# Chunk 4 of two head pairs scored in one visit on four array tiles, chunks 2 and 3 in one visit, masks ahead of the scores, one transposition for chunks 0 and 1, new ranks

## Chip, core and metric

The kernel runs on one core of a Trainium2 chip. The metric is the time of one execution on the device in microseconds (us), lower is better; it is the median of several runs. A measurement of this kernel tells a difference of about 1% from none.

## What is computed

Attention with a compressive memory, gated, and behind it a feed-forward layer with softplus, all in float32 at the interface:

```python
scores = scale * q @ k.T                       # B,H,S,D = 4,8,576,64; causal
a = exp(scores - rowmax); a /= a.sum(-1) + 1e-9
local = a @ v
mem_out = (phi(q) @ M_prev) / (phi(q) @ z_prev + 1e-6)   # phi = elu + 1
x = g * mem_out + (1 - g) * local              # g = sigmoid(beta), per head
out = softplus(x @ w_in) @ w_out               # 2304 tokens, 512 -> 2048 -> 512
```

## The kernel before

**Units, windows, chunks.** Two heads form a unit, each on 64 partitions; there are 4 batches of 4 units. A unit's 576 queries fall into window A (chunks 0 and 1, 128 queries each) and window B (chunks 2 and 3 of 128 queries, chunk 4 of 64). A batch is worked as four windows A, then four windows B; together 32 windows, numbered by `win.no`. The list `halves` has them in this order.

**One window.** `memory` (L771) computes phi(q) on ScalarE and GpSimd (L780 to L792), multiplies it with M and z on TensorE (L800) and divides on VectorE (L807 to L813). `chunks` (L503) computes the scores: for chunks 0 to 3 four float32 matmuls each, 64 rows by 64 columns of the array (L529: two heads by two halves of the queries), and behind them one bf16 matmul for each head that adds the causal mask (L540 for chunks 0 and 1 together, L544 for chunk 2 or 3). Chunk 4 holds 64 queries only: GpSimd first lays both heads' queries into a 128x128 tile `qz` with zeros elsewhere (L571), and two float32 matmuls of the full array over the 576 keys (L533) and one mask matmul (L535) follow. Then the row maximum on VectorE (L549, L552), the exponential with its row sum on ScalarE (L560, L564), the reciprocal (L595, L597), the split of the probabilities into two float16 halves on GpSimd and VectorE (L617 to L656, tile `PHL`), and a transposition of `PHL` by DMA on SyncE's queue into `PTA` or `PTB` (L630: one for each of chunks 0 to 3; L664: two for chunk 4). In windows 0 to 6 (`PEH`) the transposition is done by TensorE instead (`turned`, L715) and copied out (L724). `values` (L820) multiplies the transposed probabilities with v (L838, or L853 in windows 0 to 6), adds the memory part, and stores the window's part of x as `xhl`.

**Feed-forward layer.** A block is one batch's windows A (256 tokens) or B (320 tokens), eight blocks in all. `fill` (L898) takes a finished block through the first 7 of 16 slices of the weights (L384, `h<-xhl,w` and `h<-g,w`) while attention goes on with later windows, and stores the part sum. `rest` (L921) does the last block whole and then what is left of the others, when attention is done (L384 and L951). The weights come as 64-bit words and are decoded (`decode`, L466) by VectorE, GpSimd and ScalarE; slices 0 to 6 during the first batch, slices 7 to 15 when the tiles of attention are free. The decoding ends with L317 on GpSimd.

**What sets the order.** The functions only register operations (`op`) with an engine, a planned duration, a rank and the tiles that they read and write. `Plan.run` (L148) then goes through them as a list scheduler and writes the order of each engine, which is fixed from then on. Ranks come from the slot of a window's chunk and the tables `SLOT`, `RK`, `DEC`; `OPT` chooses the engine of some operations and the lead of the loads (`pf`). Where the plan sees a gap on TensorE in the early part, it puts matmuls on `ident` whose result is not used (L1034, "fillers" below). Scores and the transpositions on TensorE share a ring `s` of two tiles.

Of the kernel before, what the change touches and what calls it, by code (L numbers as in the profile page):

```python
# [10 lines left out]
F32 = mybir.dt.float32  # L11
# [21 lines left out]
DEC = {(0, 0): -99.18, (1, 0): -54.775, (2, 0): -197.277, (3, 0): 33.228, (4, 0): 45.246, (5, 0): 305.867, (6, 0): 52.475, (0, 1): -63.029, (1, 1): -24.184, (2, 1): -157.376, (3, 1): -80.924, (4, 1): -116.755, (5, 1): 28.921, (6, 1): -155.375}  # L33
PELO = {(0, 1), (4, 0), (2, 1), (1, 1), (2, 0), (5, 1), (3, 0), (1, 0), (4, 1)}
PHS = 10
RK = {'qz': -30.021, 'v': 36.457, 'mem': 2.9, 'prod': 16.414, 'norm': 34.649, 'r': -35.845, 'hi': -54.718, 'lo': -42.164, 'vhi': -2.071, 'vlo': -26.791, 'val': -9.765}
SLOT = {0: -12.775, 3: -66.133, 20: -22.329, 2: -24.201, 24: -137.226, 8: -16.423, 17: -94.807, 13: 41.989, 12: -82.022, 5: -57.35, 27: -24.194, 9: -20.573, 6: 30.327, 23: -262.096, 26: 144.982, 29: 129.289, 22: -36.136, 16: -1.399, 10: 75.094, 21: -4.617, 14: -88.782, 4: -45.41, 15: -80.316, 28: -160.775, 7: -8.892, 19: 14.465, 25: 7.92, 1: -139.922, 11: 30.92, 18: 74.083, 30: -27.465, 31: 120.802}
PARTS = {'A': [[0, 1]], 'B': [[2], [3], [4]]}
ORDER = [0, 1, 2, 3, 4, 5, 6]
PEH = {0, 1, 2, 3, 4, 5, 6}  # L40
OPT = {'rp': {0, 2, 3, 6, 7, 8}, 'hp': {8, 11, 12}, 'ev': {0, 6, 7, 13, 17, 19, 20, 23, 26}, 'pf': -20.780194481621944, 'hold': 1.5519182956108535, 'ab': {1, 2, 4, 5, 6, 7, 8, 9, 10, 11, 12, 13, 14, 15}, 'gp': set()}
# [53 lines left out]
class Plan:  # L95
# [5 lines left out]
    TURN = {"m": {"S": 60.0, "v": 160.0, "n": 70.0}, "f": {"v": 85.0}, "n": {"S": 30.0, "v": 80.0},  # L101
            "S": {"S": 85.0, "v": 80.0, "f": 90.0, "m": 90.0, "n": 90.0},
            "v": {"S": 80.0, "f": 90.0, "m": 90.0, "n": 90.0}}
# [44 lines left out]
    def run(self):  # L148
# [34 lines left out]
        def opens(o):  # L183
            t = 0.0
            for h in o.tiles:
                if h.ring is None or h.open:
                    continue
                if h.ring.free:
                    if h.before is not None and not h.before.open:
                        return None  # L190
                    if len(h.ring.opened) >= h.ring.bufs:
                        old = h.ring.opened[-h.ring.bufs]
# [80 lines left out]
def attn_softplus_moe(  # L273
# [25 lines left out]
    own = res.tile([128, 128], F32, name="own")  # L299
# [86 lines left out]
    def consts():  # L386
# [11 lines left out]
        P.memset(own, 0.0)  # L398
        for h in range(2):
            P.memset(own[64 * h:64 * h + 64, 64 * h:64 * h + 64], 1.0)  # L400
# [9 lines left out]
        for r in range(2):  # L410
            V.tensor_copy(cinv4[64 * r:64 * r + 64, :], cv[64 * r:64 * r + 64, :, r])
# [12 lines left out]
    def ring(pool, tag, bufs, shape, dtype=F32):  # L424
# [18 lines left out]
        "PTA": ring(al, "PTA", 2, [128, 8, 256], F16), "PTB": ring(al, "PTB", 2, [128, 18, 320], F16),  # L443
# [16 lines left out]
    QZ = [Handle(None, 0) for _ in range(2)]  # L460
    for i, h in enumerate(QZ):
        h.t = res.tile([128, 128], F32, name=f"qz{i}")
# [40 lines left out]
    def chunks(u, win, b, p, cs, ks):  # L503
# [14 lines left out]
        ss, nms, pts = (tiles(t) for t in ("s", "nm", "P"))  # L518
        l, r = R["l"].new(), R["rr"].new()

        def scores(js):
            for j in js:
                c, n, sv, qv, kv = cs[j], ns[j], ss[j](), q()[:, 130:], kk()
                cq = c * 128 - q0
                if c < 4:
                    for h in range(2):
                        rr = slice(64 * h, 64 * h + 64)
                        for e in range(0, 128, 64):
                            MM(sv[e:e + 64, h, so[j]:so[j] + n], lhsT=qv[rr, cq + e:cq + e + 64], rhs=kv[rr, :n],  # L529
# [562 lines left out]
```

## Time and profile before

| | |
|---|---|
| median of 3 runs | 611.39 us (608.29 to 611.94) |
| the profiled execution | 610.6 us |
| its span, first to last instruction | 608.8 us |
| TensorE busy | 590.4 us |
| VectorE, ScalarE, GpSimd busy | 353.0, 302.4, 173.0 us |
| granted TensorE clock, mean | 1.000 |

The busy time of an engine counts the stretches in which an instruction of it ran. In a timeline, a line merges instructions of one kind in sequence; since matmuls overlap, the cost of one line is read from its start to the start of the next, not from its own duration. A float32 matmul stands there as two instructions. In brackets stands how long the engine was idle before it and what ended that.

### The profile page before, as it was taken

The numbers are of one execution on the slowest core, as the hardware profiler recorded it, in microseconds if no ns is written. First come the engines' busy times: TensorE is split into PE (matmuls) and PEld (weight loads), VectorE is DVE, ScalarE is ACT, GpSimd is POOL, SyncE is SP. The second block draws the span as 40 slices with busy tenths as digits, with TensorE's granted clock in tenths as the row PEclk, the third lists the DMA queues.
The fourth block names the chain that finished last, engine by engine and source line by source line (L and its number), as shares of the span: only waits on it lengthen the run. The fifth ranks groups of instructions, "written<-read, shape, count | busy, mean of one in ns | idle before, by whom it ended". The sixth has DMA issues, their size and how long they took to land.

```text
span 608.8 us, 12824 instructions
## 1 busy us (share of the span) xinstructions
PE 590.4 (97%) x4866; PEld 528.5 (87%) x4866; DVE 353.0 (58%) x805; ACT 302.4 (50%) x854; POOL 173.0 (28%) x262
## 2 busy tenths in 40 slices
PE   6999999999989999989999999999999999999996
PEld 5676768787777787968799999999999999999996
DVE  6688888788877898868882776651212121212121
ACT  5758866666756785668743443432222222222221
POOL 3556533334433435326622343330000000000000
PEclk9999999999999999999999999999999999999999
DMA  8545559868999789967976643342314130522011
GB/s 314 190 125 178 181 157 220 195 195 183 205 180 210 192 187 200 177 164 163 169 123 182 214 137 106 105 145 98 105 36 133 48 132 6 167 71 70 1 44 35
DMA packets 129245, 87.41 MB, mean 144 GB/s; under 512 B 86176, under 2 KB 120992, under 8 KB 129184
## 3 DMA queue, kind: packets, MB, share of 16 engines
q1 hardware_dynamic: 129184, 86.60, 55.3%
q8 instruction: 38, 0.62, 0.4%
q14 instruction: 23, 0.19, 0.1%
HBM read 47.88 MB, written 18.22 MB: 109 GB/s over the span
## 4 chain that ended last, share of the span: by engine, by line
PE 86%; DMA 5%; DVE 4%; ACT 1%; SPq 1%; POOL 1%; issue 1%; DVEq 0%; ACTq 0%; POOLq 0%
PE h L384 43%; PE s L951 21%; PE s L529 6%; PE xp L838 4%; PE sm L800 3%; PE s L533 2%; DMA kA<-in_nat_dram 2%; PE xp L853 2%; PE xp L826 1%; PE s L544 1%; PE h L488 1%; DMA qA<-in_nat_dram 1%; PE s L715 1%; DVE nm L549 1%; DMA PTA<-PHL 1%
## 5 line engine op out<-in xcount | busy, mean ns | idle before, releaser
L384 PE MATMUL h<-xhl,w 128*128 128x256 f32 (+1 forms) x1536 | 228.1, 298 | 1.4 <-ACT pb L914 1.4
L384 PEld LDWEIGHTS h<-xhl,w 128*128 128x128 f32 x1536 | 210.4, 189 | 3.2 <-ACT pb L914 1.6
L317 DVE TENSOR_TENSOR g<-gl,g 128x256 fp32r<-128x256 f32 (+1 forms) x128 | 59.6, 470 | 162.8 <-ACT g L323 162.5
L888 ACT ACTIVATE gl<-h 128x256 f32<-128x256 f32 (+1 forms) x128 | 52.2, 410 | 179.2 <-PE h L384 176.8
L951 PE MATMUL s<-g,w 128*128 128x320 f32 (+1 forms) x948 | 139.3, 297 | 0.0
L951 PEld LDWEIGHTS s<-g,w 128*128 128x128 f32 x948 | 131.1, 188 | 0.0
L384 PE MATMUL h<-g,w 128*128 128x256 f32 (+1 forms) x588 | 87.1, 299 | 0.0
L384 PEld LDWEIGHTS h<-g,w 128*128 128x128 f32 x588 | 78.7, 189 | 0.7
L617 POOL TENSOR_SCALAR PHL<-P,rr 128x384 f16<-128x384 f32 (+3 forms) x100 | 57.4, 589 | 76.9 <-DVE rr L597 23.5
L560 ACT ACTIVATE P<-s,nm 128x256 f32<-128x256 f32 (+3 forms) x128 | 66.4, 526 | 5.2 <-DVE PHL L621 2.6
L549 DVE TENSOR_REDUCE nm<-s 128x2 f32<-128x768 f32 (+2 forms) x64 | 51.4, 818 | 13.9 <-PE s L540 7.3
L323 ACT CAST g<-gl 128x256 fp32r<-128x256 f32 (+1 forms) x128 | 55.1, 433 | 3.9
L621 DVE SCALAR_TENSOR_TENSOR PHL<-P,rr,PHL 128x384 f16<-128x384 f32 (+3 forms) x100 | 56.4, 599 | 0.8 <-POOL PHL L617 0.8
L317 POOL TENSOR_TENSOR w<-wu,w 128x512 fp32r<-128x512 f32 x23 | 30.5, 1329 | 29.2 <-ACT w L323 29.2
L353 POOL TENSOR_SCALAR wu<-wu 128x512 f32<-128x512 f32 x32 | 20.5, 643 | 43.7 <-DVE wu L349 38.3
L529 PE MATMUL s<-kB,qB 64*64 64x384 f32 (+1 forms) x256 | 31.4, 561 | 0.0
L838 PEld LDWEIGHTS <-vb 128*64 128x64 f16 x508 | 24.8, 110 | 7.1 <-issue 2.7
L360 DVE SCALAR_TENSOR_TENSOR wu<-ws,wu 128x512 int32<-128x512 int32 x32 | 26.6, 832 | 0.9
L792 POOL TENSOR_TENSOR ph<-ph,pe 128x320 f32<-128x320 f32 (+1 forms) x22 | 18.4, 838 | 30.8 <-ACT pe L784 18.9
L560 ACT ACTIVATION_READ_ACCUMULATOR P<-s,nm 128x1 f32 x128 | 25.5, 199 | 0.0
L323 ACT CAST w<-wu 128x512 fp32r<-128x512 f32 x29 | 17.9, 618 | 14.4 <-DVE wu L364 14.2
L678 POOL TENSOR_SCALAR P<-P,rr 128x256 f32<-128x256 f32 (+4 forms) x31 | 18.6, 613 | 20.5 <-DVE rr L597 10.7
(123 smaller groups left out, 643.2 us busy)
## 6 DMA issues: line engine op xcount, KB each, us to landing
ws<-in_w_in_dram SPq DMA_DIRECT2D x16, 512.0 KB, 3.6
ws<-in_w_out_dram SPq DMA_DIRECT2D x16, 512.0 KB, 3.5
va<-in_nat_dram SPq DMA_DIRECT2D x16, 320.0 KB, 3.9
xd<-xhl SPq DMA_DIRECT2D x16, 320.0 KB, 3.1
kB<-in_nat_dram SPq DMA_DIRECT2D x16, 288.0 KB, 3.8
xd<-xhl SPq DMA_DIRECT2D x16, 256.0 KB, 3.2
xhl<-xd SPq DMA_DIRECT2D x8, 512.0 KB, 4.6
xhl<-xd SPq DMA_DIRECT2D x6, 640.0 KB, 4.9
```

The source lines that it names most:

```text
L317: eng.tensor_tensor(out=out, in0=in0, in1=in1, op=ALU.subtract)
L323: A.copy(out, in_)
L360: V.scalar_tensor_tensor(out=ti(), in0=si(1), scalar=-0x40000000, in1=ti(), op0=ALU.bitwise_and, op1=ALU.bitwise_or)
L384: MM(out, lhsT=l, rhs=r, start=start and i == 0, stop=stop and i == len(pairs) - 1)
L529: MM(sv[e:e + 64, h, so[j]:so[j] + n], lhsT=qv[rr, cq + e:cq + e + 64], rhs=kv[rr, :n], start=j == js[0], stop=True, skip_group_check=True)
L549: V.tensor_reduce(out=nm()[:, 2 * j * both:2 * j * both + 2], in_=s()[:, :, so[j]:so[j] + n], op=ALU.max, axis=AX.X, negate=True)
L560: A.activation(out=pt()[:, po[j] + h * n:po[j] + h * n + n], in_=s()[:, h, so[j]:so[j] + n], func=AF.Softplus, scale=SCALE, bias=nm()[:, o ...
L617: P.tensor_scalar(out=o[:, :, 0, h, :], in0=src, scalar1=rs, scalar2=0.0, op0=ALU.mult, op1=ALU.add)
L621: V.scalar_tensor_tensor(out=o[:, :, 1, h, :], in0=src, scalar=rs, in1=o[:, :, 0, h, :], op0=ALU.mult, op1=ALU.subtract)
L838: MM(xp()[64 * h:64 * h + 64, lo:n], lhsT=vb()[:, vi, kc, 64 * h:64 * h + 64], rhs=ptw()[:, kc * 4 + t * 2 + h, lo:n], start=False, stop=( ...
L888: op("ACT", 170 + .833 * n, -1, lambda: A.activation(out=gl()[:, :n], in_=hp()[:, :n], func=AF.Softplus, scale=XSC), r=[hp], w=[gl])
L951: MM(bank(dm), lhsT=l, rhs=r, start=f == f0 and q == 0 and (not small or dm % 2 == 0), stop=f == NF - 1 and q == 2, skip_group_check=True)
```

## The change

It does six things. (1) `fours`: chunk 4 of two neighbouring units is scored in one visit of TensorE, eight float32 matmuls of 64x64 with 288 columns, the four tiles of the array taking one head of one unit each; the second unit's heads are swapped (`win.odd`). The tile `qz` and its GpSimd operation go. `values` of the even unit waits for this visit, which is planned with the odd unit's window. (2) `twos`: chunks 2 and 3 in one visit in 14 of the 16 windows B (`OPT['two']`; units 12 and 13 keep two visits); it takes both score tiles. (3) The mask matmuls stand ahead of the scores, in all visits. (4) One DMA transposition for chunks 0 and 1 in place of two, in the 12 windows A that use DMA; `PTA` gets the shape 128x12x128. (5) Windows 10 and 11 add phi's two parts by accumulating matmuls (`PHS` 10 to 12), as windows 0 to 9 do; one block's casts of `g` go from ScalarE to GpSimd (`gp`), two operations of window 30 and 31 from GpSimd to ScalarE. (6) The tables of ranks, the planned durations and the planned costs of switching are new.

```diff
-PHS = 10
+PHS = 12
-PARTS = {'A': [[0, 1]], 'B': [[2], [3], [4]]}
+PARTS = {'A': [[0, 1]], 'B': [[2], [3]]}
...
+    def fours(wins, ks):
+        ss = [R["s"].new() for _ in wins]
...
+        def scores():
+            for s in ss:
+                MM(s()[:, 1, 224:288], lhsT=identb, rhs=mask4, start=True, stop=False, skip_group_check=True)
+            for i in (1, 0):
+                for h in range(2):
+                    rr = slice(64 * h, 64 * h + 64)
+                    for s, w in zip(ss, wins):
+                        o = 64 * (h ^ w.odd)
+                        MM(s()[o:o + 64, i, :288], lhsT=w.q()[rr, 130 + 256:130 + 320],
+                           rhs=w.k()[rr, 288 * i:288 * i + 288], start=i == 0, stop=True, skip_group_check=True)
...
+    def twos(win, ks):
+        ss = [R["s"].new() for _ in range(2)]
...
+        def scores():
+            for c, s in zip((2, 3), ss):
+                for h in range(2):
+                    MM(s()[:, h, c * 128:c * 128 + 128], lhsT=identb, rhs=mask, start=True, stop=False,
+                       skip_group_check=True)
+            for c, s in zip((2, 3), ss):
+                n = c * 128 + 128
+                for h in range(2):
+                    rr = slice(64 * h, 64 * h + 64)
+                    for e in range(0, 128, 64):
+                        MM(s()[e:e + 64, h, :n], lhsT=win.q()[rr, 130 + n + e - 384:130 + n + e - 320],
+                           rhs=win.k()[rr, :n], start=False, stop=True, skip_group_check=True)
...
-                else:
-                    for i in range(2):
-                        MM(sv[:, i, :288], lhsT=win.qz(), rhs=kv[:, 288 * i:288 * i + 288], start=True, stop=True)
-            if m == 1:
-                MM(sv[:, 1, 224:288], lhsT=identb, rhs=mask4, start=False, stop=True, skip_group_check=True)
...
-                op("POOL", 470, k + RK["qz"], lambda: P.tensor_tensor(
...
-                op("SP", (1230, 1250, 1650, 2600)[c], k + RK["lo"], lambda j=j, c=c, nk=nk: SY.dma_start_transpose(
...
+                if c == 1:
+                    op("SP", 1450, k + RK["lo"], lambda: SY.dma_start_transpose(out=ptw(), in_=phl()[:, 0:1536]),
+                       r=[(phl, i) for i in range(8)], w=[(ptw, c)], dma=2520)
...
+        if w == "B" and win.odd:
+            ks = [key(0), key(1)]
+            both = fours([prev[1], win], ks)
+            chunks(*prev, [4], ks[:1], both[0])
+            chunks(u, win, b, p, [4], ks[1:], both[1])
+            slot += 2
+            values(*prev, slot + RK["val"], xhs[2 * b + 1])
+        pre = twos(win, [key(0), key(1)]) if w == "B" and u.no in OPT["two"] else None
```

Of the tables, `OPT` shows the kind of change: `'pf': -20.78` becomes `-15.88` (the loads' lead in ranks), `'hold'` 1.55 becomes 0.0.

**TensorE, second batch, chunk 4.** Before, each unit's chunk 4 has a visit of its own; the first of the four, with the mask's matmuls of chunk 3 ahead of it and the feed-forward matmuls behind it (`kB` and `qB` are keys and queries of a window B, `s` a score tile, `w0` to `w6` slices of weights).

```order
L544 MATMUL s_1924<-mask_66,identb_64 128x128
L533 MATMUL s_1935<-kB_1069,qz0_101 128x288 x2
L535 LDWEIGHTS identb_64
L535 MATMUL s_1935<-mask4_67,identb_64 128x64
L384 MATMUL h_1943<-g_1702,w0_94 128x320 x3
```

Now both units of the pair stand in one visit, the masks ahead, the matmuls of the two units by turns.

```order
L506 LDWEIGHTS identb_64
L506 MATMUL s_1846<-mask4_67,identb_64 128x64
L506 LDWEIGHTS identb_64
L506 MATMUL s_1848<-mask4_67,identb_64 128x64
L512 MATMUL s_1846<-kB_1178,qB_1168 64x288
L512 MATMUL s_1848<-kB_1317,qB_1302 64x288
L512 MATMUL s_1846<-kB_1178,qB_1168 64x288
L512 MATMUL s_1848<-kB_1317,qB_1302 64x288
L512 MATMUL s_1846<-kB_1178,qB_1168 64x288
L512 MATMUL s_1848<-kB_1317,qB_1302 64x288
L512 MATMUL s_1846<-kB_1178,qB_1168 64x288
L512 MATMUL s_1848<-kB_1317,qB_1302 64x288
```

Sixteen visits of two matmuls have become eight visits of eight, each writing to two score tiles.

**SyncE's queue, windows A of the third batch.** Before (`PTA` transposed probabilities, `kA`, `qA`, `va` loads for windows A, `part` the stored part sums, `xd` the stored x), each window has two transpositions, and the third load of keys stands in front of the first pair of them.

```order
L873 DMA xd_81<-xhl_2305 256x1x320
L989 DMA kA_2698<-in_nat_dram 128x256
L630 DMA_TRANSPOSE PTA_2702<-PHL_2653 128x4x128
L630 DMA_TRANSPOSE PTA_2702<-PHL_2653 128x8x128
L992 DMA va_2750<-in_nat_dram 128x640
L915 DMA part_80<-pb_2755 128x256
L915 DMA part_80<-pb_2760 128x256
L987 DMA qA_2782<-in_nat_dram 128x386
L630 DMA_TRANSPOSE PTA_2792<-PHL_2734 128x4x128
L630 DMA_TRANSPOSE PTA_2792<-PHL_2734 128x8x128
```

Now there is one for each window, and the fourth load of keys stands ahead of the first of them.

```order
L1024 DMA kA_2680<-in_nat_dram 128x256
L663 DMA_TRANSPOSE PTB_2528<-PHL_2552 128x16x128
L1024 DMA kA_2740<-in_nat_dram 128x256
L1027 DMA va_2822<-in_nat_dram 128x640
L660 DMA_TRANSPOSE PTA_2834<-PHL_2664 128x12x128
L908 DMA xd_80<-xhl_2184 256x1x320
L950 DMA part_79<-pb_2866 128x256
L950 DMA part_79<-pb_2878 128x256
L1022 DMA qA_2895<-in_nat_dram 128x386
L660 DMA_TRANSPOSE PTA_2918<-PHL_2722 128x12x128
```

The transpositions of chunks 0 and 1 are 12 rows in all where they were 24, and all four loads of keys of a batch now precede them. The count of fillers on TensorE (L1034 before) goes from 22 to 39, all in the first batch.

## Rows read from the trace of the kernel before

**Rows 1.** The page: busy time of each engine and its share of the span.

```profile
PE 590.4 (97%) x4866; PEld 528.5 (87%) x4866; DVE 353.0 (58%) x805; ACT 302.4 (50%) x854; POOL 173.0 (28%) x262
```

**Rows 2.** Windows: stretch, its us, busy PE, PEld, DVE, ACT, POOL; clock, DMA.

```profile
15.00:50.00 35.00, 33.12 (x261) 23.05 (x262) 26.48 (x66) 24.60 (x77) 19.87 (x35) 1.00 0.52 172
50.00:100.00 50.00, 49.24 (x405) 36.09 (x402) 44.70 (x105) 37.02 (x106) 23.74 (x35) 1.00 0.62 176
100.00:150.00 50.00, 48.46 (x410) 40.62 (x410) 40.74 (x98) 31.96 (x99) 18.77 (x30) 1.00 0.79 190
150.00:200.00 50.00, 46.82 (x484) 39.46 (x483) 40.64 (x105) 33.49 (x110) 19.52 (x32) 1.00 1.00 201
...
250.00:300.00 50.00, 48.45 (x450) 40.47 (x447) 38.98 (x99) 34.73 (x106) 20.57 (x33) 1.00 0.80 165
```

**Rows 3.** Waits of TensorE: us in total, times, longest.

```profile
PE s L529 <- DMA kA<-in_nat_dram: 4.6, 4, 1.7
PE s L529 <- DMA qA<-in_nat_dram: 1.5, 1, 1.5
PE h L384 <- ACT pb L914: 1.4, 1, 1.4
```

**Rows 4.** Timeline of TensorE, second batch, visits of chunks 3, 4 and 2.

```profile
130.59 1.09 PE L529 MATMUL s<-kB,qB 64*64 64x512 f32 x8
131.61 0.29 PE L544 MATMUL s<-mask,identb 128*128 128x128 bf16 x2
131.73 1.19 PE L533 MATMUL s<-kB,qz 128*128 128x288 f32 x4
132.76 0.19 PE L535 MATMUL s<-mask,identb 128*128 128x64 bf16 x1
132.79 3.32 PE L384 MATMUL h<-g,w 128*128 128x320 f32 x21
136.04 0.88 PE L529 MATMUL s<-kB,qB 64*64 64x384 f32 x8
136.85 0.29 PE L544 MATMUL s<-mask,identb 128*128 128x128 bf16 x2
136.94 2.44 PE L384 MATMUL h<-g,w 128*128 128x320 f32 x15
139.31 1.09 PE L529 MATMUL s<-kB,qB 64*64 64x512 f32 x8
```

**Rows 5.** The page's groups: weight loads of L384 (last figures: idle before).

```profile
L384 PEld LDWEIGHTS h<-xhl,w 128*128 128x128 f32 x1536 | 210.4, 189 | 3.2 <-ACT pb L914 1.6
```

**Rows 6.** Timeline of TensorE, first batch: fillers, and matmuls of the memory.

```profile
15.88 1.60 PE L1034 MATMUL sm<-ident 128*128 128x122 f32 x12 [2.32 <-DVE mA L813]
17.32 1.03 PE L488 MATMUL h<-wu,ident 128*128 128x512 f32 x2
...
22.23 0.39 PE L800 MATMUL sm<-qA,ph 128*128 128x130 f32 x2
22.45 0.39 PE L800 MATMUL sm<-qA,pe 128*128 128x130 f32 x2
```

**Rows 7.** Timeline of SyncE's DMA queue, windows A of the third batch.

```profile
171.76 1.64 SPq L630 DMA_TRANSPOSE PTB<-PHL  x1
...
184.83 2.63 SPq L630 DMA_TRANSPOSE PTA<-PHL  x2
```

**Rows 8.** Groups by form: what follows a score tile of chunk 4.

```profile
L552 DVE TENSOR_REDUCE nm<-s 128x1 f32<-128x576 f32 x16 | 12.1, 755 | 4.1 <-PE s L535 4.0
L564 ACT ACTIVATE P<-s,nm 128x576 f32<-128x576 f32 x16 | 11.8, 740 | 1.5 <-DVE PHL L651 0.5 <-DVE PHL L656 0.2
```

**Rows 9.** Timelines: last value matmuls, then the decoder's end and the matmul behind it.

```profile
330.06 1.72 PE L838 MATMUL xp<-PTB,vb 128*64 128x320 f16 x28
...
400.84 1.30 POOL L317 TENSOR_TENSOR w<-wu,w 128x512 fp32r<-128x512 f32 x1
...
402.65 4.76 PE L384 MATMUL h<-xhl,w 128*128 128x320 f32 x36
```

More of the change, by code (lines that the diff above doesn't have):

```diff
@@ L188, in opens @@
                 if h.ring.free:
-                    if h.before is not None and not h.before.open:
+                    if h.before is not None and not h.before.open and h.before not in o.tiles:
                         return None
-                    if len(h.ring.opened) >= h.ring.bufs:
-                        old = h.ring.opened[-h.ring.bufs]
+                    i = len(h.ring.opened) + sum(g.ring is h.ring and not g.open for g in o.tiles[:o.tiles.index(h)])
+                    if i >= h.ring.bufs:
+                        old = h.ring.opened[i - h.ring.bufs]
                         if old.left:
@@ L543, in scores @@
                 else:
-                    MM(sv[:, h, e - 128:e], lhsT=identb, rhs=mask, start=False, stop=True, skip_group_check=True)
+                    MM(sv[:, h, x - 128:x], lhsT=identb, rhs=mask, start=True, stop=False, skip_group_check=True)
+            for j in js:
+                c, n, qv, kv = cs[j], ns[j], q()[:, 130:], kk()
+                cq = c * 128 - q0
+                for h in range(2):
+                    rr = slice(64 * h, 64 * h + 64)
+                    for e in range(0, 128, 64):
+                        MM(sv[e:e + 64, h, so[j]:so[j] + n], lhsT=qv[rr, cq + e:cq + e + 64], rhs=kv[rr, :n],
+                           start=False, stop=True, skip_group_check=True)
@@ L914, in fill @@
             op("ACT", 160 + .833 * n, -1, lambda o=o, pb=pb: A.copy(pb()[:, :n], o()[:, :n]), r=[o], w=[pb])
[L915 removed]
+            op("SP", 490, 0, lambda dm=dm, pb=pb: SY.dma_start(out=part[:, dm, t0:t0 + n], in_=pb()[:, :n]),
                r=[pb], w=[(PART[bi], dm)], dma=1.45 * n)
@@ L1004, in attn_softplus_moe, with key @@
         memory(u, win, p, k0 + (RK["mem"] if hi_ else .5), hi_ < PHS)
-        for grp in PARTS[w]:
-            chunks(u, win, b, p, grp, [slot + j + SLOT.get(slot + j, 0.0) for j in range(len(grp))])
+        def key(j):
+            return slot + j + SLOT.get(slot + j, 0.0)
+        if w == "B" and win.odd:
[6 more added lines that the diff above has]
+        pre = twos(win, [key(0), key(1)]) if w == "B" and u.no in OPT["two"] else None
+        for i, grp in enumerate(PARTS[w]):
+            chunks(u, win, b, p, grp, [key(j) for j in range(len(grp))], pre and pre[i])
             slot += len(grp)
@@ L1010, in attn_softplus_moe @@
             xhs[bi] = R["xhl"].new()
-        values(u, win, b, p, slot + RK["val"], xhs[bi])
+        if w == "B" and not win.odd:
+            prev = (u, win, b, p)
+        else:
+            values(u, win, b, p, slot + RK["val"], xhs[bi])
         if p == NP - 1 and bi < LASTB:
```

104 lines of the change are left out of this document (49 added, 55 removed).

## Prediction

> **What bounds the kernel now.** I read four views in this order: busy time by engine, the same in stretches of time, TensorE's waits, and the timelines of the places that the change touches. In the first, TensorE is busy for 590.4 us of a span of 608.8, 97%; the next engine, VectorE, has 353.0 [rows 1]. The reader is to see that what TensorE does, and in what order, is the time, and that no other engine has a comparable total. The second view tells the stages apart [rows 2]. From 15 to 100 us, the first batch, TensorE is idle for 1.88 + 0.76 us, but part of its busy time there is fillers. From 100 to 300 us its idle time in the stretches shown is 1.54, 3.18 and 1.55 us, 6.3 us together. VectorE is busy for 44.7 of 50 us in the first batch and about 40 of 50 later: no limit by itself, but too near to give a large further gain away. The clock reads 1.00, the level of 2.4 GHz, in each stretch, so I use one duration per operation. The third view names who makes TensorE wait: loads of keys for 4.6 us, of queries for 1.5, and a copied-out part sum for 1.4 [rows 3]. So two things can shorten the run: less work on TensorE, and earlier loads. Behind the last value matmuls, which start at 330.06 us [rows 9], there is no attention left; a gain must be made before that point, and must not be lost after it.
>
> **Chunk 4 in pairs.** Before, chunk 4 of a unit costs TensorE 1.06 us, from 131.73 to 132.79, its mask included [rows 4]; a pair costs 2.12. For the new visit I take the price of tiled score matmuls from chunks 2 and 3. Chunk 2 has four matmuls of 384 columns on four tiles: 0.81 us from its start to its mask. Chunk 3 has 512 columns: 1.02 us. So 128 columns on all four tiles cost 0.21 us, 1.64 ns per column, and 0.18 us is fixed. The eight new matmuls are two rounds of 288 columns: 576 x 1.64 ns + 0.18 = 1.12 us. Two masks add 0.03 us each, as from 132.76 to 132.79. What the trace doesn't show is the way out: the next full-array weights follow tiles directly, where a mask stood between. That costs between nothing and one weight load, 0.189 us [rows 5]; as part of a load overlaps, I take the middle, 0.09. The visit is 1.27 us, the gain 0.85 us a pair, 0.75 to 0.94, and for 8 pairs **-6.8 us** (-7.5 to -6.0).
>
> The trace shows the two row groups of a chunk 2 or 3 running side by side, 0.81 us for four matmuls [rows 4]; but there each head writes a bank of its own. In `fours` the two heads of a unit write one bank at the same time, on different partitions. The Trainium skill, TensorEngine Tiling (Array Packing), section Restrictions and Gotchas, says that different row tiles cannot access the same PSUM bank simultaneously. By that rule the two would go one after the other, and this term would vanish (the first rival below); by the rows of chunk 2 it stands. No row here has two row groups in one bank.
>
> **Chunks 2 and 3 in one visit.** Apart, they cost 0.90 us (136.04 to 136.94) and 1.14 us (130.59 to 131.73), and each entry loses a little: 15 feed-forward matmuls take 2.37 us before an entry, where 21 without one take 3.25, so 0.05 us [rows 4]. Together 2.14 us. In one visit: masks 0.09 + 0.12, 896 columns x 1.64 ns = 1.47, fixed 0.18 once, way out 0.09: 1.95 us. The gain is 0.19 us, 0 to 0.28; with the wait for two free score tiles in mind I take 0.17, times 14 visits **-2.4 us** (-3.9 to 0).
>
> **Masks first in the other visits.** Sixteen visits for chunks 0 and 1 and four single ones keep their work, save the entry of 0.05 us, and gain the way out, 0 to 0.19: **+0.8 us** (-1.0 to +2.8).
>
> **Memory matmuls.** Windows 10 and 11 get four more matmuls of 0.22 us, from 22.23 to 22.45 [rows 6]: **+0.9 us**. Two GpSimd additions go, and sixteen that built `qz`, while seven casts move there; GpSimd is busy for 173 us [rows 1], and these lie beside TensorE's work.
>
> **The first batch.** Fillers rise from 22 to 39. One costs 0.24 us: six, twelve instructions, from 15.88 to 17.32 [rows 6]. All stand ahead of the first batch's feed-forward output. If they stand where TensorE would wait anyway they cost nothing; if nothing waits, 17 x 0.24 = 4.1 us; and if the waits grow with their count, the 2.6 us of idle time of 15 to 100 us grow by 17/22, 2.0 us more. I take **+2.5 us** (0 to +6.1), nearer to the middle, because the first unit's chunk 4 now waits for the second unit's loads and memory work, while its three chunks could go one after another before.
>
> **One transposition.** Two transpositions of chunks 0 and 1 take SyncE's queue 2.63 us; one of the same 12 blocks, that of chunk 2, takes 1.64 [rows 7]. So the queue gets 1 us back for each of 12 windows, just where it issues one entry behind the other without a gap and where TensorE's waits for loads fall. All four loads of keys of a batch now also stand ahead of its first `PTA` transposition, as the order shows. Of the 6.3 us idle between 100 and 300 us I take back half, **-3.0 us** (-6.3 to 0). What comes late next is the transposed result: it now waits for chunk 1, where chunk 0 went ahead; but its values need both.
>
> **The sum.** -6.8 - 2.4 + 0.8 + 0.9 + 2.5 - 3.0 = -8.0 us. The profiled execution took 610.6 us, 1.8 more than its span, so it would be 602.6. The median of the runs is 611.39, 0.8 above the profiled one; the forecast on that footing is **603.4 us**. All lower ends together would give -17.8 us (593.6), all upper ends +3.8 (615.2).
>
> **Rivals.** *Row groups don't share a bank.* Then a pair's tiles take 1152 columns x 1.64 ns + 0.18 = 2.07 us, with masks and way out 2.22, and the term is +0.8 instead of -6.8: 611.0 us. For it speaks only that no row shows the case; against it, that each column group still writes two banks, as in chunk 2. 0.08.
>
> *The gain is hidden by the decoder.* Slices 7 to 15 are decoded when attention's tiles are free, and the last but one piece ends at 402.14 us, only 0.5 us ahead of the matmul at 402.65 that reads it [rows 9]. If the chain from there back doesn't move with TensorE, at most the 0.5 us and the small terms survive: about 610 us. For it speaks this margin; against it, that the chain starts from the last transpositions, which move forward with the scores, and that in the new order 18 feed-forward matmuls more than before stand behind the last values. 0.18.
>
> *Score tiles run out* (slower). A visit of `fours` or `twos` takes both tiles. The first is free again when its maximum and its exponential are done, 0.755 + 0.740 us [rows 8] and the small steps between; the second exponential adds 0.74. Where less work than this, 2 to 3 us, stands before the next scores or transposition, TensorE waits. Later batches have feed-forward matmuls there, the first has few: behind its second `fours` stand five fillers and then transpositions. If the 22 visits lose 0.7 us each, that is +15.4 us, 618.8 us. It decides from 8.0/22 = 0.36 us a visit on. Against it: the order mostly puts 3 us and more between. 0.12.
>
> **How the numbers follow.** The forecast has 0.62. Its own range, from the two uncertain terms (first batch, loads), is 598 to 608.5 us. About 1% is what a measurement can tell, 605.3 us on the one side and 617.5 on the other. Of the forecast's 0.62 some 0.50 lies below 605.3 and 0.12 within; the hidden gain and the shared bank add 0.26 within; of the slower rival 0.08 lies above 617.5 and 0.04 within. So faster 0.50, same 0.42, slower 0.08. The range of 8 in 10 is 597 to 612.5: it takes in the first two rivals and leaves out the third, and some of both tails.
>
> **What would show each step.** In the new timeline, from the first tile of a chunk-4 pair to the next visit about 1.2 us; 2.2 would be the shared bank. A visit of chunks 2 and 3 about 1.95 us from its first mask. `PTA` transpositions 12 times, at 1.6 us or less. TensorE's waits for keys and queries nearer to 3 us than to 6. The feed-forward output of the first batch (the first `h<-g,w` of the timeline) no more than 3 us later than before. The last value matmuls at about 322 us, and from there to the end no longer than now. The forecast is wrong if waits of TensorE on score tiles, on VectorE or ScalarE, together pass 8 us, or if a gap opens before the matmul that reads the last decoded slice.

## The result and the profile after

The changed kernel takes 604.94 us (median of 7 runs, 604.48 to 607.35) where the kernel before took 611.39 in the same comparison (608.29 to 614.84). The ratio is 0.9898, with a 95% interval of 0.9874 to 0.9921: faster by about 1%, and clear of no change. The forecast of 603.4 was 1.5 us too low, and the measurement lies in its range. The profiled execution took 604.73 us with a span of 602.9, 5.9 less than before.

The page of the changed kernel, busy time of each engine, answers to [rows 1]:

```profile
PE 587.9 (98%) x4972; PEld 529.0 (88%) x4972; DVE 358.5 (59%) x807; ACT 299.2 (50%) x848; POOL 172.8 (29%) x247
```

TensorE's busy time fell by 2.5 us only, less than half of the 5.9 us, and it has 106 instructions more; the rest is idle time. The windows of the changed kernel tell where (columns as in [rows 2]):

```profile
15.00:50.00 35.00, 33.22 (x272) 24.07 (x272) 30.81 (x74) 24.18 (x74) 23.01 (x35) 1.00 0.56 192
50.00:100.00 50.00, 47.16 (x386) 35.04 (x385) 41.36 (x91) 33.53 (x92) 18.97 (x28) 0.97 0.46 144
100.00:150.00 50.00, 49.31 (x473) 40.93 (x472) 44.29 (x104) 36.60 (x118) 21.80 (x35) 1.00 0.99 211
150.00:200.00 50.00, 50.00 (x525) 41.75 (x524) 43.36 (x112) 35.20 (x114) 21.89 (x34) 1.00 0.98 213
200.00:250.00 50.00, 49.14 (x463) 40.96 (x462) 43.77 (x104) 35.79 (x112) 20.48 (x29) 1.00 0.92 190
250.00:300.00 50.00, 49.14 (x480) 40.44 (x483) 42.15 (x104) 33.01 (x99) 22.27 (x32) 1.00 0.85 168
```

Read the second and third figures of a row together: from 100 to 300 us TensorE is idle for 0.69 + 0 + 0.86 + 0.86 = 2.4 us. In the kernel before the row that sums the same four stretches is this, 200.00 - 193.55 = 6.45 us idle:

```profile
sum 200.00, PE 193.55 PEld 160.66 DVE 164.32 ACT 135.74 POOL 82.22; mean PE 48.39 PEld 40.16 DVE 41.08 ACT 33.93 POOL 20.55
```

So 4.0 us of idle time went there. The first batch went the other way: from 50 to 100 us the idle time rose from 0.76 to 2.84 us, and the granted clock fell to 0.97. TensorE's waits in the changed kernel, us in total, times, longest, name both sides:

```profile
PE sm L1083 <- DVE mA L841: 3.1, 2, 1.9
...
PE s L579 <- DMA qA<-in_nat_dram: 1.5, 2, 0.9
PE xp L874 <- DMA PTA<-PHL: 0.7, 1, 0.7
PE s L579 <- DMA kA<-in_nat_dram: 0.7, 1, 0.7
```

The waits for keys fell from 4.6 to 0.7 us [rows 3], those for queries stayed, and the wait for a part sum is gone. The largest is now that of the fillers (L1083) for the reader of their own tile, a division on VectorE; in the kernel before, fillers (L1034) waited about as long for the same reader:

```profile
PE sm L1034 <- DVE mA L813: 2.7, 2, 2.3
```

The timeline of TensorE in the second batch, with one visit of a chunk-4 pair (L506, L512) and one of chunks 2 and 3 (L527, L534), answers to [rows 4]:

```profile
126.46 0.23 PE L506 MATMUL s<-mask,identb 128*128 128x64 bf16 x2
126.62 1.20 PE L512 MATMUL s<-kB,qB 64*64 64x288 f32 x16
127.75 0.49 PE L828 MATMUL sm<-qA,ph 128*128 128x130 f32 x2
...
136.10 0.39 PE L527 MATMUL s<-mask,identb 128*128 128x128 bf16 x4
136.42 1.73 PE L534 MATMUL s<-kB,qB 64*64 64x384 f32 x16
138.08 0.44 PE L854 MATMUL xp<-ident,mB 128*128 128x128 f32 x2
```

Start to start (ends are modelled), the pair takes 127.75 - 126.46 = 1.29 us, 1.13 of it the tiles; chunks 2 and 3 take 138.08 - 136.10 = 1.98 us. A row says x16 where eight matmuls stand in the program, since each float32 matmul is recorded twice.

The timeline of TensorE in the first batch, and then at the last value matmuls:

```profile
78.57 1.20 PE L512 MATMUL s<-kB,qB 64*64 64x288 f32 x16
81.69 1.38 PE L1083 MATMUL sm<-ident 128*128 128x122 f32 x10 [1.92 <-DVE mA L841]
...
83.23 1.94 PE L747 MATMUL s<-ident,P 128*128 128x128 f32 x8
84.97 0.64 PE L828 MATMUL sm<-qA,ph 128*128 128x130 f32 x2
...
94.24 1.67 PE L383 MATMUL h<-g,w 128*128 128x256 f32 x12
...
321.83 1.72 PE L874 MATMUL xp<-PTB,vb 128*64 128x320 f16 x28
```

Two windows of the same place (columns as in [rows 2]; the eighth figure is the granted clock):

```profile
80.00:84.00 4.00, 2.25 (x16) 2.08 (x17) 2.86 (x8) 2.83 (x8) 2.39 (x3) 0.88 0.73 182
84.00:88.00 4.00, 4.00 (x22) 3.51 (x20) 2.07 (x7) 1.39 (x3) 0.69 (x1) 0.69 0.57 214
```

Behind the first batch's second chunk-4 pair (78.57) TensorE waits 1.92 us. VectorE's timeline shows for what: it takes the row maxima of the pair's two score tiles ahead of the division that the filler waits for.

```profile
79.82 1.42 DVE L588 TENSOR_REDUCE nm<-s 128x1 f32<-128x576 f32 x2
81.16 0.48 DVE L841 SCALAR_TENSOR_TENSOR mA<-sm,sc,a 128x256 f32<-128x256 f32 x1
```

Soon after this wait the clock is granted at its lower level, 1.2 GHz, for a part of the two windows: eight transpositions take 84.97 - 83.23 = 1.74 us, and a memory matmul 0.43 us instead of 0.22 [rows 6]. In the kernel before, eight transpositions at the same place took 1.02 us, to 80.81:

```profile
79.79 1.09 PE L715 MATMUL s<-ident,P 128*128 128x128 f32 x8
```

Three marks give the balance of the span. The first feed-forward output (`h<-g,w`) comes at 94.24 us, 2.04 later than before (92.20). From there to the last value matmuls it takes 227.59 us instead of 237.86, 10.27 less. From there to the end it takes 2.33 more: the 18 feed-forward matmuls that now stand behind the values, at 0.126 us each 2.3 us. 2.04 - 10.27 + 2.33 = -5.9 us. The tail is accounted for, the gain lies between the first two marks, and a loss lies ahead of them.

### The profile page after: what moved, and what is told of

It is laid out like the page before. It is cut to its first block, busy times and chain, and to the rows that moved or that the text cites. A ratio compares the mean times of both kernels' runs of the same rounds, so it can differ in the third digit from the quotient of the medians.

```text
span 602.9 us, 12965 instructions
## 1 busy us (share of the span) xinstructions
PE 587.9 (98%) x4972; PEld 529.0 (88%) x4972; DVE 358.5 (59%) x807; ACT 299.2 (50%) x848; POOL 172.8 (29%) x247
## 4 chain that ended last, share of the span: by engine, by line
PE 86%; DMA 3%; DVE 1%; ACT 0%; POOL 0%; issue 0%; SPq 0%; DVEq 0%; POOLq 0%
PE h L383 45%; PE s L986 21%; PE xp L874 4%; PE s L534 3%; PE sm L828 3%; PE s L579 2%; PE xp L854 1%; PE s L512 1%; PE s L747 1%; DMA PTA<-PHL 1%; DMA kA<-in_nat_dram 1%; PE xp L888 1%; DMA qA<-in_nat_dram 1%; PE h L483 1%; DMA PTB<-PHL 1%; PE s L527 0%
## 5 line engine op out<-in xcount | busy, mean ns | idle before, releaser
L383 PE MATMUL h<-xhl,w 128*128 128x256 f32 (+1 forms) x1536 | 225.6, 298 | 0.0
L316 DVE TENSOR_TENSOR g<-gl,g 128x256 fp32r<-128x256 f32 (+1 forms) x128 | 63.1, 497 | 154.9 <-ACT g L322 153.6
L646 POOL TENSOR_SCALAR PHL<-P,rr 128x384 f16<-128x384 f32 (+3 forms) x100 | 61.3, 626 | 86.8 <-DVE rr L626 25.5
L596 ACT ACTIVATE P<-s,nm 128x128 f32<-128x128 f32 (+3 forms) x128 | 66.5, 525 | 2.6
L322 ACT CAST g<-gl 128x256 fp32r<-128x256 f32 (+1 forms) x121 | 51.6, 432 | 3.4
L585 DVE TENSOR_REDUCE nm<-s 128x2 f32<-128x768 f32 (+2 forms) x64 | 50.0, 816 | 3.3 <-PE s L579 2.8
L355 DVE TENSOR_SCALAR wu<-wu 128x512 int32<-128x512 int32 x32 | 19.0, 592 | 13.2 <-POOL wu L352 13.2
L534 PE MATMUL s<-kB,qB 64*64 64x384 f32 (+1 forms) x224 | 24.3, 549 | 0.0
L591 ACT ACTIVATE nm<-nm 128x2 f32<-128x2 f32 (+2 forms) x64 | 12.8, 199 | 23.0 <-DVE nm L585 14.3
```

The costliest lines, as they stand in the source:

```text
L316: eng.tensor_tensor(out=out, in0=in0, in1=in1, op=ALU.subtract)
L322: A.copy(out, in_)
L383: MM(out, lhsT=l, rhs=r, start=start and i == 0, stop=stop and i == len(pairs) - 1)
L534: MM(s()[e:e + 64, h, :n], lhsT=win.q()[rr, 130 + n + e - 384:130 + n + e - 320], rhs=win.k()[rr, :n], start=False, stop=True, skip_group_ ...
L585: V.tensor_reduce(out=nm()[:, 2 * j * both:2 * j * both + 2], in_=s()[:, :, so[j]:so[j] + n], op=ALU.max, axis=AX.X, negate=True)
L596: A.activation(out=pt()[:, po[j] + h * n:po[j] + h * n + n], in_=s()[:, h, so[j]:so[j] + n], func=AF.Softplus, scale=SCALE, bias=nm()[:, o ...
```

## The experiments

Twelve kernels ran; ratios are to the kernel before. Eleven are the changed kernel or edits of it, so the one to compare with is its own repetition.

**The changed kernel again.**

> The changed kernel once more, as the reference for the three runs beside it. Both theories: ratio to the kernel before 0.987 to 0.992, span near 602.9 us.

605.91 us, 0.9908 (0.9887 to 0.9929); span 603.5, idle time from 100 to 300 us 2.87, first output at 94.32 us, last values at 322.45. The profiled executions of the changed kernel and of its repetition agree within 0.6 us in these marks; less than that is not read below. More can differ, too: the spans of the repetition's six executions run from 602.3 us, at a granted clock of 0.999, to 605.6 at 0.992. A mark below tells what happened in one profiled execution; only the median speaks for the kernel.

**Does the pair's gain come from four tiles side by side?** The pair's eight matmuls are written unit by unit instead of by turns.

```diff
-            for i in (1, 0):
-                for h in range(2):
-                    rr = slice(64 * h, 64 * h + 64)
-                    for s, w in zip(ss, wins):
+            for s, w in zip(ss, wins):
+                for i in (1, 0):
+                    for h in range(2):
+                        rr = slice(64 * h, 64 * h + 64)
```

> The changed kernel with the eight matmuls of a pair of chunk 4 written unit by unit, so that only two of the four tiles can run at a time; same matmuls, same order otherwise. Theory 1: the matmuls of a visit take 1152 columns x 1.64 ns + 0.18 = 2.07 us where they take 1.13 now, 8 times 0.94 = +7.5 us, span about 610.4, so that the whole gain of the change is gone. Rival (the gain comes from the new order and the loads, chunk 4 is hidden): span within 1.5 us of the changed kernel.

605.12 us, 0.9894 (0.9872 to 0.9917). The timeline of TensorE at a pair:

```profile
126.94 1.21 PE L512 MATMUL s<-kB,qB 64*64 64x288 f32 x16
128.08 0.49 PE L828 MATMUL sm<-qA,ph 128*128 128x130 f32 x2
```

1.14 us, the same as by turns. The premise was wrong, that writing one unit's four matmuls first would leave the other unit's two tiles idle: eight matmuls on four tiles take the time of two rounds in either order. So this run did not take the four tiles apart, and the doubled pairs below are the test of the term. That the time equals two rounds, 576 columns, also shows that the two row groups run side by side where they write one bank on different partitions.

**Does TensorE's time in a visit count in full?** The pair's eight matmuls are done twice; the first pass is overwritten.

```diff
+            for i in (1, 0):
+                for h in range(2):
+                    ...
+                        MM(s()[o:o + 64, i, :288], ..., start=True, stop=True, skip_group_check=True)
             for s in ss:
                 MM(s()[:, 1, 224:288], lhsT=identb, rhs=mask4, start=True, ...)
```

> The changed kernel with the eight matmuls of each pair of chunk 4 done twice (the first time into the same score tiles ahead of the masks, then overwritten), so that a visit costs TensorE what two visits cost before: 1.29 + 0.97 = 2.26 us. Theory 1 (TensorE sets the pace everywhere): +0.97 x 8 = +7.8 us, span about 611. Rival (from the second batch on loads and transposed results set the pace as well, and part of TensorE's time is hidden): +2 to +5 us, span 605.5 to 608.5, with fewer waits for DMA.

615.04 us, 1.0058 (1.0037 to 1.0078), span 613.1. The timeline of TensorE at a pair:

```profile
227.54 1.20 PE L510 MATMUL s<-kB,qB 64*64 64x288 f32 x16
228.68 0.23 PE L513 MATMUL s<-mask,identb 128*128 128x64 bf16 x2
228.84 1.20 PE L519 MATMUL s<-kB,qB 64*64 64x288 f32 x16
229.97 2.32 PE L383 MATMUL h<-g,w 128*128 128x320 f32 x14
```

The visit takes 229.97 - 227.54 = 2.43 us, 1.14 more than 1.29. The expectation had 0.97, but the first pass pays its own fixed part (1.14 to the masks). Eight times 1.14 is 9.1 us; against the repetition the median grew by 9.1 and the span by 9.6. So work added to TensorE here is paid in full, and the rival that the decoder hides what attention gains or loses falls.

**Is it one visit that chunks 2 and 3 gain by?** The two loops of the joint visit become one, so that the array goes from masks to tiles twice.

```diff
             for c, s in zip((2, 3), ss):
                 for h in range(2):
                     MM(s()[:, h, c * 128:c * 128 + 128], lhsT=identb, rhs=mask, ...)
-            for c, s in zip((2, 3), ss):
                 n = c * 128 + 128
```

> The changed kernel with masks and scores of chunk 2 ahead of masks and scores of chunk 3 inside the joint visit, so that the array changes between full and tiled twice more. Theory 1: a visit takes 0.21 + 0.81 + 0.21 + 1.02 = 2.25 us instead of 1.98, 14 times 0.27 = +3.8 us, span about 607. Rival (hidden): the visit grows by the same, the span by less than 1.5 us.

607.70 us, 0.9937 (0.9912 to 0.9963), span 604.7. The timeline of TensorE at a joint visit:

```profile
214.81 0.28 PE L527 MATMUL s<-mask,identb 128*128 128x128 bf16 x2
215.03 0.88 PE L533 MATMUL s<-kB,qB 64*64 64x384 f32 x8
215.84 0.28 PE L527 MATMUL s<-mask,identb 128*128 128x128 bf16 x2
216.05 1.09 PE L533 MATMUL s<-kB,qB 64*64 64x512 f32 x8
217.07 1.72 PE L873 MATMUL xp<-PTB,vb 128*64 128x320 f16 x28
```

2.26 us against 1.99 for the same visit of the repetition (214.51 to 216.50): +0.27 us for one more change between the full array and tiles, 3.8 us for 14 visits. The median rose by 1.8 us and the span by 1.2; the first output came 0.7 us earlier (93.60), since in this execution the clock stayed at 1.00 behind the wait at 80 us, and from 113 us to the last values the kernel lost 1.8. The price of a change is shown; that all 14 of them reach the end is not.

**What do masks ahead of the scores cost?** In all visits the mask matmuls stand behind the scores again.

```diff
-                MM(s()[:, 1, 224:288], lhsT=identb, rhs=mask4, start=True, stop=False, ...)
...
+                MM(s()[:, 1, 224:288], lhsT=identb, rhs=mask4, start=False, stop=True, ...)
```

> The changed kernel with the mask matmuls behind the scores in all visits; the order of all engines is otherwise the same. Theory 1 (the time is the sum of TensorE's work and waits): a visit for chunks 0 and 1 falls from 1.13 to 1.01 us (16 of them, -1.9), a joint visit of chunks 2 and 3 from 1.98 to 1.92 (14, -0.8), a pair of chunk 4 from 1.29 to 1.23 (8, -0.5), four single visits by 0.07 (-0.3): together -3.5 us, span about 599.4, ratio to the changed kernel 0.994. Rival (the other engines set the pace and TensorE's saving comes back as waits): within 1 us of the changed kernel.

607.46 us, 0.9932 (0.9905 to 0.9959), span 607.7. No gain; the expectation is refuted. The profiled execution is the longest of six (their spans run from 603.0 to 607.7), so what follows says what its visits cost, and not what the median rose by. The joint visit itself is shorter, 1.91 us (118.39 to 120.30), but the matmuls ahead of it pay more to enter, and the stretch from 117 to 145 us takes 27.82 us where the repetition takes 27.79. Two visits of chunks 0 and 1 in the third batch can be laid side by side, since the same work stands around them. The timeline of TensorE in the repetition:

```profile
174.77 0.27 PE L854 MATMUL xp<-swap,mB 128*128 128x128 f32 x1
174.88 0.38 PE L568 MATMUL s<-mask,identb 128*128 128x256 bf16 x2
175.19 0.88 PE L579 MATMUL s<-kA,qA 64*64 64x128 f32 x16
...
179.85 0.18 PE L781 MATMUL sm<-least,mean 128*128 128x1 bf16 x1
```

and with the masks behind:

```profile
177.98 0.27 PE L854 MATMUL xp<-swap,mB 128*128 128x128 f32 x1
178.19 0.88 PE L572 MATMUL s<-kA,qA 64*64 64x128 f32 x16
179.00 0.39 PE L576 MATMUL s<-mask,identb 128*128 128x256 bf16 x2
...
182.89 0.18 PE L781 MATMUL sm<-least,mean 128*128 128x1 bf16 x1
```

5.08 us against 4.91 with two visits between the marks; two other visits of the same batch give 8.25 against 8.15. So masks ahead cost 0.05 to 0.08 us in a visit of chunks 0 and 1, about 1.1 us for 16, and nothing measurable in the joint ones. This execution did not get that back, because by 113 us it had lost more. The timeline of TensorE at one place, with the masks behind:

```profile
105.94 0.88 PE L572 MATMUL s<-kA,qA 64*64 64x128 f32 x16 [1.83 <-DMA kA<-in_nat_dram]
```

and its window:

```profile
108.00:112.00 4.00, 4.00 (x27) 4.00 (x27) 2.23 (x9) 1.93 (x9) 0.25 (x1) 0.71 1.37 268
```

A wait of 1.83 us for a load (0.94 in the repetition), then the lower clock again: the marks behind it stand 3.1 us later (116.74 against 113.61), of which 1.0 had been lost by the first output (95.29 against 94.32). The shorter visits did not bring the scores ahead of their keys: TensorE came to this place 0.7 us later than in the repetition, and the keys' load was issued 1.3 us later (100.85 against 99.56). Whether the other executions lost their time in the same way is not shown.

**Two transpositions again**, of four and eight blocks, issued one behind the other.

```diff
-                    op("SP", 1450, ..., lambda: SY.dma_start_transpose(out=ptw(), in_=phl()[:, 0:1536]),
+                    op("SP", 1450, ..., lambda: [SY.dma_start_transpose(out=ptw()[:, a:z], in_=phl()[:, 128 * a:128 * z]) for a, z in ((0, 4), (4, 12))],
```

> The changed kernel with two DMA transpositions for chunks 0 and 1 again (of 4 and 8 of the 12 blocks), at the place of the one; the order is otherwise the same. Theory 1 (the shorter queue of SyncE gave TensorE its loads earlier): a window's transpositions take the queue about 1 us more, TensorE's waits for loads and transposed results behind 100 us rise from 2.9 us to 5 to 6.5, span 605.5 to 607. Rival (it is the new place of the loads in the order that did it): waits and span within 1 us of the changed kernel.

606.83 us, 0.9925 (0.9899 to 0.9952), span 605.3: 1.8 us more than the repetition, all of it there by the last values (324.35 against 322.45). The median is 0.9 us above the repetition's. On SyncE's queue the line of these transpositions has min/median/max, ns, of 24 here:

```profile
L660 SPq DMA_TRANSPOSE PTA<-PHL x24: 1188/1260/2034, 111.8 to 274.4; - x24
```

and of 12 in the changed kernel:

```profile
L660 SPq DMA_TRANSPOSE PTA<-PHL x12: 1415/1598/2146, 111.5 to 271.1; - x12
```

Two of 1.26 us are 2.52 against 1.60, 0.9 us of the queue for a window. The sum row of TensorE's four stretches from 100 to 300 us shows 4.15 us idle where the repetition has 2.87:

```profile
sum 200.00, PE 195.85 PEld 162.79 DVE 171.80 ACT 139.18 POOL 83.99; mean PE 48.96 PEld 40.70 DVE 42.95 ACT 34.80 POOL 21.00
```

**One transposition in the kernel before**, and nothing else of the change but the new layout of `PTA`, which the value matmuls then read; it stands at the place of the later of the two.

```diff
-        "PTA": ring(al, "PTA", 2, [128, 8, 256], F16)
+        "PTA": ring(al, "PTA", 2, [128, 12, 128], F16)
...
+                        win.seen = getattr(win, "seen", 0) + 1
+                        if win.seen == 2:
+                            SY.dma_start_transpose(out=ptw(), in_=phls[j]()[:, 0:1536])
+                        return
```

> The kernel before with one DMA transposition for chunks 0 and 1, at the place of the later of the two; nothing else is changed. Theory 1 (the queue): TensorE's waits for loads behind 100 us fall from 6.3 us to 3 to 4.5, span 605.5 to 607.5, ratio 0.995 to 0.998. Rival (place of the loads): no change, ratio 0.999 to 1.001.

607.56 us, 0.9937 (0.9914 to 0.9960), span 606.8, 2.0 less than before; last values at 327.96 us, 2.1 earlier. The same sum row:

```profile
sum 200.00, PE 196.17 PEld 162.10 DVE 168.27 ACT 137.40 POOL 81.95; mean PE 49.04 PEld 40.53 DVE 42.07 ACT 34.35 POOL 20.49
```

3.8 us idle instead of 6.45. Put in alone, the one transposition is worth 2.0 us between the profiled executions and 3.6 between the medians (607.56 against 611.13); taken out alone, 1.8 and 0.9. Its sign is the same each time, its size is known to no better than 1 to 4 us of the gain of 6. In the idle time from 100 to 300 us it shows as 2.6 and 1.3 of the 4.0 us that went; that the rest belongs to what else moved the loads is not shown.

**Part sums stored from ScalarE's queue**, 28 issues fewer on SyncE's. Is it the room on SyncE's queue or the transfers themselves?

```diff
-            op("SP", 490, 0, lambda dm=dm, pb=pb: SY.dma_start(out=part[:, dm, t0:t0 + n], in_=pb()[:, :n]),
+            op("SP", 490, 0, lambda dm=dm, pb=pb: A.dma_start(out=part[:, dm, t0:t0 + n], in_=pb()[:, :n]),
```

> The changed kernel with the 28 stores of part sums issued by ScalarE, right behind the copies that make them, instead of by SyncE. Theory 1 (SyncE's queue, busy without a gap in stretches, makes TensorE wait behind 100 us): about 0.45 us each leaves the queue, the 2.9 us of idle time between 100 and 300 us fall to 1 to 2 us, span 602 to 603. Rival (the DMA engines themselves, 0.96 to 0.99 busy between 100 and 200 us, are the limit, not the queue): span within 0.7 us of 603.5, or higher by what ScalarE's issue costs.

606.08 us, 0.9930 (0.9903 to 0.9958), span 603.0; idle time from 100 to 300 us 3.0 against 2.87. Freeing that much of the queue gave nothing that the median shows, so plain room on it is hardly what the transposition's gain consists of. In the changed kernel the DMA share from 100 to 200 us is 0.98 to 0.99, which speaks for the transfers; it is not shown.

This execution shows another thing. All fillers stand in it, the wait of 1.92 us stands at its place (81.97), and up to 76 us its marks are within 0.15 us of the repetition's. But the clock did not fall behind the wait:

```profile
80.00:84.00 4.00, 2.02 (x21) 1.80 (x18) 3.12 (x9) 2.58 (x7) 2.40 (x3) 1.00 0.63 172
84.00:88.00 4.00, 3.92 (x28) 2.72 (x28) 2.84 (x9) 2.60 (x6) 0.69 (x1) 1.00 0.60 223
```

Its first output comes at 92.97 us, 1.35 earlier than in the repetition, where these two windows read 0.73 and 0.85. So that is the price of the fall there. It is not in every execution: a wait of 1.9 to 2.0 us stands at this place in all twelve profiled executions of the changed kernel and its edits, and in four of them the clock stays at 1.00 behind it.

**Without fillers.**

```diff
-            if o.eng == "PE" and o.spare:
+            if False and o.eng == "PE" and o.spare:
```

> The changed kernel without its 39 filler matmuls (their results are not used); the order of all engines is otherwise the same. Theory A (fillers stand where work is ready and delay it, and are themselves waiting for a tile at 80 us): the first h<-g,w comes 1 to 4 us earlier than at 94.2 us and the span falls by the same, 599 to 602. Theory B (they hold the clock): the granted clock falls to its lower level in more of the first batch, scores and transpositions there take twice as long, the first h<-g,w comes 2 to 10 us later, span 605 to 613.

605.87 us, 0.9897 (0.9874 to 0.9920), span 604.3. The first output comes at 92.25 us, 2.07 earlier, although the clock is 0.90 from 15 to 50 us instead of 1.00. At 158 us 1.6 us of the lead is left, at 182 us it is a lag of 0.9. The timeline of TensorE shows where one part goes:

```profile
171.69 1.69 PE L874 MATMUL xp<-PTB,vb 128*64 128x320 f16 x27 [1.61 <-DMA PTB<-PHL]
```

The values wait for transposed probabilities, in total 3.8 us in four waits. The four chunk-4 transpositions before that took SyncE's queue 6.52 us (from 164.86) instead of 5.32 in the repetition. What TensorE gained early it returned here in waits for transfers.

**Only the early fillers**: the first 18 of 39 stay.

```diff
-            if o.eng == "PE" and o.spare:
+            if o.eng == "PE" and o.spare and (o.start < 25000.0):
```

> The changed kernel with the first 18 of its 39 filler matmuls, those of the first 25 us; the order is otherwise the same. Theory 1 (the later fillers delay ready work, the early ones keep the clock up): the clock stays at its upper level at 15 to 21 us, the first h<-g,w comes at 91 to 92 us (94.3 with all, 92.3 with none). What follows tells two theories of the later batches apart: if TensorE alone sets the pace there, the span falls by as much, to 600.5 to 601.5 us; if the queue of transposed results and loads has no room left (as the run without fillers hints), most of it returns as waits for DMA and the span is 602.5 to 604 us.

603.73 us, 0.9890 (0.9862 to 0.9919), span 601.5. The clock is 1.00 from 15 to 50 us, and the first output comes at 92.54, 1.8 earlier than in the repetition; at 113 us 1.3 are left, at the last values (320.48) 2.0. So the 21 late fillers carry 1.8 us of the first batch's loss. The wait at 80 us is not theirs. Without them the next instruction waits there, for the same division:

```profile
81.94 0.16 PE L781 MATMUL sm<-least,mean 128*128 128x1 bf16 x1 [2.01 <-DVE mA L841]
```

And the clock still falls, to 0.81 and 0.76 in the two windows from 80 to 88 us, so it is not the fillers that cause that fall. This has the lowest median of all, but its interval holds the changed kernel's ratio.

**Early fillers with the part stores moved, and with masks behind for chunks 0 and 1 too.** Both edits above together, then a third.

> Both edits: the first 18 fillers alone, and the part sums' stores from ScalarE. Theory 1 (queue): what the run with early fillers gives back is kept here, span 599.5 to 601.5 us. Rival (DMA engines): as the run with early fillers, within 0.7 us.

> Both edits and, for chunks 0 and 1 alone, the masks behind the scores (1.04 us a visit instead of 1.13, 16 visits, 1.4 us of TensorE). Theory 1: 1 us below the run with both edits, 598.5 to 600.5 us. Rival (loads and transposed results set the pace in the windows A): no gain over it, or a loss where a load is met earlier, as in the run with all masks behind.

605.87 us, 0.9928 (0.9903 to 0.9953), and 604.67 us, 0.9908 (0.9879 to 0.9937). The first has its first output at 91.01 us, with the clock at 1.00 behind the wait: 1.5 earlier than with early fillers alone, where it fell, and 2.0 earlier than with the part stores alone, where it did not fall and the late fillers stand. So both prices come out twice: 1.4 to 1.5 us for the fall of the clock, 1.8 to 2.0 for the late fillers. It was 1.9 us ahead of the repetition at 113 us and 0.25 behind at 186 us: what was gained early was returned by the first window of the third batch, in waits for transposed probabilities. The second was 2.2 to 3.4 us behind from 205 us on in its profiled execution, the longest of its six: a wait of 2.47 us for a transposed result stands there, and a granted clock of 0.67 from 204 to 208 us. Neither beats the changed kernel.

## Why the prediction was nearly right, and what was mis-sized

The mechanism held: TensorE's order and idle time are the time, and both sides of it gained. What failed is the size of one term, the first batch, by a fall of the clock that was put at nothing. The terms, as put and as measured:

- *Chunk 4 in pairs, -6.8.* Before 2.12 us a pair, now 1.29: 0.83 x 8 = -6.6. The fixed part, the columns and the way out came as estimated (1.27). The bank rule that was weighed there would have given 2.22 us; with the tiles at 1.13 us it does not hold here, where the two row groups write one bank on different partitions. The doubled pairs show that such time counts in full.
- *Chunks 2 and 3 in one visit, -2.4.* 1.98 against 2.14 us: 0.16 x 14 = -2.2. The price of one more change of the array, +0.27, says what the term consists of.
- *Masks first, +0.8.* About +1.1 for the visits of chunks 0 and 1. Within its bounds, but one reading in it was wrong: the 0.05 us for an entry came from 15 matmuls that end at a visit on tiles and 21 that were taken to end without one, and in [rows 4] those 21 end at such a visit too (136.04). No row there shows what an entry costs.
- *Memory matmuls, +0.9.* Four more at their old price; not separately measured.
- *The first batch, +2.5.* This is the step that failed in size. The first output is 2.04 us later, although two pairs (-1.7) and joint visits (-0.6) already gained ahead of it, and masks first lost about 0.3 in four visits: the loss is 2.04 + 2.3 - 0.3 = 4.0 us. (What else stands ahead of the mark nearly cancels: one visit of chunks 0 and 1 fewer, 1.0 us, and four memory matmuls more, 0.9.) The fillers were priced about right: the 21 late ones, some 5 us at 0.24 each, brought the first output 1.8 to 2.0 us later, in two pairs of executions; five of them (81.69) stand between the wait at 80 us and the transpositions. What the prediction put at nothing is the clock. It took one duration per operation, since the clock read 1.00 in each stretch of the kernel before. Behind the wait at 80 us it fell, eight transpositions and four memory matmuls lost 0.7 us each, and the first output came 1.4 to 1.5 us later than in executions where it did not fall. That is what the 4.0 have more than the 2.5. Fillers and clock are 3.2 to 3.5 of the 4.0; the rest is open, also because it was not measured what the 22 fillers of the kernel before cost. The wait itself is new, since no wait of TensorE is listed from 60 us to the first output of the kernel before. It stands without the fillers too, and VectorE takes the pair's two maxima right ahead of the division that ends it; that the pair causes it was not tested.
- *Loads and one transposition, -3.0.* Idle time from 100 to 300 us fell by 4.0, 1.3 to 2.6 of it by the one transposition. The waits for keys fell to 0.7 us, and the wait for a part sum went too, though the term was about loads.

The terms as measured give -6.6 - 2.2 + 1.1 + 0.9 + 4.0 - 4.0 = -6.8 us against -5.9 of the span; what makes up the 0.9 us between them is open. So the forecast missed by its first batch, 1.5 us too low there, and by luck the loads, 1.0 us better than put, made up for a part of it.

The rivals: the shared bank fell by the pair's 1.29 us. The decoder's hiding fell, as the time behind the last values grew by just the 18 matmuls that moved there, and doubled pairs reached the end whole. Score tiles did not run out: no wait of TensorE on a score tile's reader stands in the list of its waits. But the place that this rival named, behind the second `fours` of the first batch, is where TensorE's longest wait behind the start came, for VectorE; TensorE's waits on VectorE and ScalarE are 6.9 us in all, under the 8 that were the sign, and 7.2 in the kernel before. The tests named beforehand came out so: the pair 1.29 (1.2), the joint visit 1.98 (1.95), 12 `PTA` transpositions of 1.60 (1.6), keys and queries 2.2 us (nearer 3 than 6), first output +2.04 (3 or less), last values 321.83 (322), no wait listed behind 300 us. One did not: the time from there to the end was to be no longer and is 2.33 us longer, by the 18 matmuls that the prediction itself had put there.

What stays open: the last half us of the first batch; why the clock falls behind the same wait in some executions and not in others; why a lead won before 113 us is kept with early fillers alone and lost without any fillers or with the part stores moved as well; and whether the transposition's gain is its transfer or its place among the loads, as emptying the queue of stores did not help.

## What to carry to other kernels

Price a tiled visit as a fixed part plus columns, and count the changes between the full array and tiles, here 0.27 us each time there and back: joining visits is worth that, and filling all four tiles is worth the columns. Removing work from an engine that is 98% busy pays in full only where nothing else is late next; in two of the kernels here what was saved ahead of a stretch with a DMA share of 0.97 to 1.03 came back as waits for transposed results within 75 us. Before adding work as filler, look at whether the engine would wait at that place: here the late fillers brought the first output 1.8 us and more later, and did not keep the clock up. And a wait of TensorE has a second price, the lower clock behind it, which a profile at 1.00 does not show: here 1.4 us, in some executions and not in others.

## What was not expected of the hardware

Of the two orders tried in which matmuls are issued to the four tiles, neither is faster: by turns 1.13 us, unit by unit 1.14. A mask ahead of or behind the tiled scores of a joint visit moves the price of the change from one side of the visit to the other rather than away (1.98 or 1.91 us for the visit, with 27.79 or 27.82 us for the stretch around it). And a short wait can cost more than itself: in stretches of 4 us that begin some 2 us behind waits of 1.92 and 1.83 us the granted clock is 0.69 and 0.71, and matmuls of 0.22 us take 0.43. It need not: the wait of 2.32 us in the kernel before [rows 6] left the clock at 1.00, and so did the wait at 80 us in four executions of twelve.
